# Forgetting attention with a channel mix on one core: a first part of 192 queries, two first chunks of 128 tokens, idle matmuls in vacant banks, one transpose less a head, seven banks at the end

## The chip, the cores and the metric

The kernel runs on one core of one Trainium2 chip. The metric is the device time of one execution in microseconds (us); a kernel's time is the median of several executions. The engines named here are PE (TensorE: matrix products), PEld (its loads of the stationary operand), DVE (VectorE), ACT (ScalarE), POOL (GpSimd) and SP (SyncE, which issues the DMAs).

## What is computed

Causal attention with a forgetting bias for 8 batches, 8 heads, 576 positions and a head size of 64, and then a channel mix over the 512 features of all heads:

```
cum    = cumsum(maximum(s, 0))
scores = where(causal, -1e9, q @ k.T / sqrt(D) + minimum(-(cum_i - cum_j), 0))
attn   = exp(scores - max);  attn = attn / (sum(attn) + 1e-9)
x      = attn @ v                          # as (batch, position, 512)
xk     = mu_k * x + (1 - mu_k) * x_prev    # x_prev: x of the position before
xr     = mu_r * x + (1 - mu_r) * x_prev
k      = maximum(xk @ w_k, 0)              # 512 -> 1024
out    = sigmoid(xr @ w_r) * ((k * k) @ w_v)
```

## The kernel before

**Attention.** The 576 queries of a batch fall into five tiles: tile 0 has 64 queries, tiles 1 to 4 have 128 each, and tile t sees 64, 192, 320, 448 or 576 keys. A *visit* is a pair of heads of one batch with some tiles. Batch 0 is visited in two parts, A (tiles 0, 1, 2: the first 320 queries) for four pairs and then Z (tiles 3, 4) for the four; batches 1 to 7 are visited with all tiles. For each head and tile PE makes the scores in a bank of tag "s" (L667 in plain fp32 in the first four visits; L678 in two passes, with k split into KH and KL, in the rest), DVE adds the bias and reduces (L695, into W), ACT takes the exponent (L713), and POOL normalizes W in place (L726). PE then transposes the normalized weights in pieces of 64 or 128 keys into banks "t" (L772, `turn`), in `block` (a block of 128 keys, all tiles that see them) and `halves` (the 64 keys that tile t alone sees in its own block). ACT and DVE evict them as ph and pl (L799, L803, and L831, L838, L846 for halves). The products with the values (L889 plain for batch 0, L903 split for the others) go to bank "po" and are copied to xT (L924, L931, L935), which is stored to DRAM as x_d.

**Channel mix.** It runs in chunks of CT = 256 tokens, 18 of them. A chunk loads x (L1130), mixes it with the shifted x on ACT and DVE (L977, L986), splits it into xh and xl (L1005, L1009), and makes hidden products with w_k (L1038: four groups of two 128-row blocks of features, 24 matmuls a group), evicted by ACT and DVE as r, a square in place, kh and kl (L1050, L1060, L1065, L1067), then the gate with w_r (L1080, sigmoid L1092) for each 128 tokens, and the output with w_v (L1105, product with the gate L1116, store). `mix(0)` makes xk for the hidden products, `mix(1)` xr for the gate. Each of these products takes a bank of tag "m".

**Banks.** PSUM has eight banks of 512 columns: m 2, t 2, s 2, po 1, and one (xp) for other use.

**Order.** Nothing is emitted as the code above is called. Each call of `pe`, `act`, `dve`, `pool` and `dma` records a task with its engine, a cost, its reads and writes and a due time (class `Plan`). `forward` places the tasks in a list schedule: of the engines' ready tasks the one that starts next and is due first. `backward` makes due times from the schedule, and after some passes the best order is emitted as it is, so each engine's instructions are in a fixed order that the planner chose. Batch 0's early chunks become due as soon as their tokens are there, so the planner fills PE with mix products between the attention's.

**Idle matmuls.** Where the planner sees PE with nothing to do for more than `GAP`, it puts in matmuls that compute nothing (L359: the identity in bf16, 128x192, into columns 320:512 of one "s" bank). They stand until the first split score product (`plan.busy_from`).

Of the kernel before, what the change touches and what calls it, by code (L numbers as in the profile page):

```python
# [14 lines left out]
BF16 = mybir.dt.bfloat16  # L15
# [38 lines left out]
class Plan:  # L54
# [10 lines left out]
    TICK, ENOUGH = 10240 / 3, 3400.0  # L65
    GAP = 170.0

# [53 lines left out]
    def forward(self, due):  # L121
# [11 lines left out]
        engines = {t[0] for t in self.tasks}  # L133
        free = dict.fromkeys(engines, 0.0)
        coming = {e: [] for e in engines}
        ready = {e: [] for e in engines}
# [7 lines left out]
        def clock(s):  # L144
            return 1.0 if ticks.get(int(s // self.TICK) - 1, 0.0) >= self.ENOUGH else 2.0

        def count(s, ns, x):
            while ns > 0.0:
                k = int(s // self.TICK)
                part = min(ns, (k + 1) * self.TICK - s + 1e-3)  # L150
                ticks[k] = ticks.get(k, 0.0) + x * part / ns
                s, x, ns = s + part, x - x * part / ns, ns - part

        while len(order) < n:
            best = None
# [11 lines left out]
            if (  # L167
                waiting
                and f <= s
                and not (ready["PE"] or coming["PE"] and coming["PE"][0][0] < f + self.GAP)  # L170
            ):
                emits.setdefault(len(order), []).append(self.idle)
                ns = 82.0 * clock(f)
                count(f, ns, 192.0)
                free["PE"] = f + ns
                continue
# [108 lines left out]
def forgetting_attention_then_channel_mix(  # L285
# [22 lines left out]
    NF = DF // P  # L308
    CT = 256
    NCHUNK = B * S // CT  # L310
    SCALE = 1.0 / math.sqrt(D)
# [38 lines left out]
    def dma(emit, reads, writes, ns):  # L350
# [5 lines left out]


    idle = bank(1, "s", 2)
    plan.idle = lambda: nc.tensor.matmul(  # L359
        idle.get()[:, 320:512],  # L360
        ident.ap.bitcast(BF16)[:, 0:P],
        ident.ap.bitcast(BF16)[:, 0:192],
        start=True,
# [11 lines left out]

    early = [w[:3] for w in weights]
    for w in weights:
        early.append([])
        for t in range(3):
            c = sum(KN[:t])  # L380
            early[-1].append(fixed(w[NQ - 1].ap[:, c : c + KN[t]]))
        w[NQ - 1].last = early[-1]

    for w in early:
        nc.gpsimd.memset(w[0].ap[64:P], 0.0)

# [157 lines left out]

    ALL, A, Z = tuple(range(NQ)), (0, 1, 2), (3, 4)
    first = []
# [78 lines left out]
    def scores(b, h, tiles, G, KH, KL):  # L625
# [35 lines left out]
        def products(t, m, i, k0, w, W):  # L661
# [14 lines left out]
            for x, K in enumerate((KH, KL) if KL is not None else ()):  # L676
                y = pe(
                    lambda x=x, K=K: nc.tensor.matmul(  # L678
                        ps.get()[:m, :w],
                        G.get()[:, q0 : q0 + m],  # L680
                        K.get()[:, k0 : k0 + w],
                        start=x == 0,
                        stop=x == 1,
                    ),
                    [(G, x) for x in range(2)] + [(K, x) for x in range(2)], [ps], w, m,
                )
                if plan.busy_from is None:
                    plan.busy_from = y

# [33 lines left out]

        def normalize(t, m, n, W):
            pool(
                lambda: nc.gpsimd.tensor_scalar(  # L726
                    out=W.ap[:m, :n],
                    in0=W.ap[:m, :n],
                    scalar1=rinv.get()[:m, t : t + 1],
                    scalar2=1.0,  # L730
                    op0=ALU.mult,
                    op1=ALU.mult,
                ),
                [rinv], [(W, i) for i in range(3)], n, 244,
            )
# [19 lines left out]
        dve(lambda: nc.vector.reciprocal(rs(rinv), rs(rinv)), [], [rinv], 8 * len(tiles))  # L755
        for t in tiles:
            normalize(t, QN[t], KN[t], pt[t])
        return pt

    def weighted(j, pt, V, xT, tiles, plain):  # L760
# [55 lines left out]
        def halves(ps, at, k0, k1):  # L816


            for t in range(k0, k1 + 1):
                turn(ps, at + P * (t - k0), t, t * P, 64)  # L820
            n = 64 * (k1 + 1 - k0)
# [33 lines left out]
        if len(tiles) == NQ:  # L855
            ps = bank(1, "t", 2)
            halves(ps, 0, 1, NQ - 1)
            ps = bank(1, "t", 2)
            block(ps, 0, 0)
            ps = bank(1, "t", 2)  # L860
            halves(ps, 384, 0, 0)
            block(ps, 0, 1)
            ps = bank(1, "t", 2)
            block(ps, 0, 2)
            block(ps, 256, 3)
            rest = ps
        elif tiles[0] == 0:
            ps = bank(1, "t", 2)
            halves(ps, 256, 0, 0)
            block(ps, 0, 0)  # L870
            ps = bank(1, "t", 2)
            halves(ps, 0, 1, 2)
            block(ps, 256, 1)
        else:
            ps = bank(1, "t", 2)
            block(ps, 0, 0, 2)
            ps = bank(1, "t", 2)
            block(ps, 0, 2)
            ps = bank(1, "t", 2)
            halves(ps, 0, 3, 4)  # L880
            block(ps, 256, 3)
        lo, ot = 64 * j, 64 * (1 - j)
# [72 lines left out]

    def channel_mix(ch, start, span):
        t0 = ch * CT
        segs = []
        t = t0
        while t < t0 + CT:  # L960
# [3 lines left out]
            t = e  # L964
        st = {}

        def at(x):
# [29 lines left out]
        def splits(c, xm, hi, lo):  # L997
# [3 lines left out]
            def src():  # L1001
                return xm.get().rearrange("p (c x) -> p c x", c=2)

# [21 lines left out]
        def hidden(fp):  # L1025
# [3 lines left out]
            hi, lo = st[0]  # L1029
            ps = bank(1, "m", 2)  # L1030
            for u in range(2):
                f = 2 * fp + u
                for c in range(NC):
                    for n, (w, x) in enumerate(
                        ((0, hi), (0, lo), (1, hi))
                    ):
                        pe(
                            lambda u=u, f=f, c=c, n=n, w=w, x=x: nc.tensor.matmul(  # L1038
# [6 lines left out]
                            [(weight["k", c, f // 4], w), (x, c)], [ps], CT,  # L1045
                        )

            r = sbuf([P, 2, CT], "r")
            act(
                lambda: nc.scalar.activation(r.get(), ps.get(), AF.Relu, scale=0.5),  # L1050
                [ps], [r], 2 * CT,
            )
            fs = slice(2 * fp, 2 * fp + 2)
            kh, kl = st["kh"], st["kl"]

            def sq():
                return ps.get().rearrange("p (u x) -> p u x", u=2)

            dve(
                lambda: nc.vector.scalar_tensor_tensor(  # L1060
# [12 lines left out]
        def gate(tt):  # L1073
            hi, lo = st[1]
            ts = slice(tt * P, (tt + 1) * P)
            ps = bank(1, "m", 2)
            for c in range(NC):
# [19 lines left out]
        def output(tt):  # L1097
            kh, kl = st["kh"], st["kl"]
            ts = slice(tt * P, (tt + 1) * P)
            ps = bank(1, "m", 2)  # L1100
            for f in range(NF):
# [52 lines left out]

    EARLY = QS[3]
    visits = [(0, hp, x) for x in (A, Z) for hp in range(NP)]
# [80 lines left out]
    for n, (b, hp, tiles) in enumerate(visits):  # L1237
# [19 lines left out]
        while done_chunks < NCHUNK:  # L1257
            end = (done_chunks + 1) * CT - 1
            if end % S >= there[end // S]:
                break  # L1260

            chunk_due = max(chunk_due + CHUNK, due + 2 * step + (MARGIN if end >= S else EARLY_MARGIN))
            channel_mix(done_chunks, chunk_due, CHUNK)
            done_chunks += 1
# [40 lines left out]
```

## Time and profile before

| | us |
|---|---|
| median of 3 runs (lowest, highest) | 902.78 (902.77, 905.7) |
| the profiled execution | 903.98 |
| its span | 902.2 |
| PE busy in the span | 877.5 (97%) |
| ACT busy | 679.4 (75%) |
| DVE busy | 672.1 (74%) |
| POOL busy | 493.5 (55%) |
| hidden products on PE, xh part (L1038) | 233.7 |
| transposes on PE (L772) | 184.1 |
| idle matmuls on PE (L359) | 20.6 |

The profile is of one execution, and the span runs from the first instruction to the last. 1.8 us of the execution lie outside it. An engine's busy time is the union of its instructions' time. Matmuls overlap in PE's pipeline, so a group's mean duration is more than its pace; the pace is read from how far the starts of neighbours stand apart. The chain that ended last is 32% PE, 5% each DVE and ACT; the rest of the span lies before the part that the profile follows back.

### The profile page before, as it was taken

Reading aid. Unit: us, or ns where it says so; the run is one execution under the profiler, and the core shown is the slowest. Engines: PE = TensorE matmul, PEld = TensorE weight load, DVE = VectorE, ACT = ScalarE, POOL = GpSimd, SP = SyncE. Lnnn points to the kernel's source line nnn. Section 1 sums busy time; section 2 is a strip of 40 time slices with the busy share of each in tenths; the row PEclk is TensorE's granted clock in tenths of the full one; section 3 lists DMA queues with packets and bytes.
Section 4 is the critical chain, followed back from the end, with each engine's and each line's share of the span. In section 5 each row is a group of like instructions: output and inputs, shape, how many; then the busy total and the mean of one; then the engine's idle time right before and its main releaser. Section 6 shows DMA issues by size and latency. Waiting matters only on the chain. (4 is left out here: it accounts for less than half of the span.)

```text
span 902.2 us, 18627 instructions
## 1 busy us (share of the span) xinstructions
PE 877.5 (97%) x5664; PEld 760.2 (84%) x5664; DVE 672.1 (74%) x2385; ACT 679.4 (75%) x1810; POOL 493.5 (55%) x856
## 2 busy tenths in 40 slices
PE   8889999999999999999999999999999999998998
PEld 6658778888889898989898989898888888887886
DVE  6887979979877888778878686877777778445431
ACT  4888989989978897789868687877787877335331
POOL 4796998896666576457666466554655551100000
PEclk9999999999999999999999999999999999999999
DMA  7688745563453354234443334342534220101100
GB/s 255 197 254 248 231 136 166 148 174 99 149 154 112 124 144 131 87 97 142 131 130 112 111 109 150 100 127 78 154 81 142 81 85 15 42 31 36 47 24 23
DMA packets 63637, 109.59 MB, mean 121 GB/s; under 512 B 10160, under 2 KB 25008, under 8 KB 63536
## 3 DMA queue, kind: packets, MB, share of 16 engines
q1 hardware_dynamic: 63536, 108.40, 40.0%
q8 instruction: 44, 0.72, 0.3%
q14 instruction: 57, 0.47, 0.2%
HBM read 89.33 MB, written 19.04 MB: 120 GB/s over the span
## 5 line engine op out<-in xcount | busy, mean ns | idle before, releaser
L1038 PE MATMUL m<-xh,w_k 128*128 128x256 f32 x1152 | 233.7, 288 | 2.6 <-DVE kl L1067 2.4
L713 ACT ACTIVATE W<-W,nm 64x64 f32<-64x64 f32 (+4 forms) x320 | 179.7, 562 | 41.8 <-DVE nm L695 35.6
L1105 PE MATMUL m<-w_v,kh 128*128 128x512 f32 x576 | 198.2, 403 | 0.0
L1038 PEld LDWEIGHTS m<-xh,w_k 128*128 128x128 f32 x1152 | 186.7, 190 | 5.4 <-DVE kl L1067 3.1
L772 PE MATMUL t<-ident,W 128*128 128x128 f32 (+1 forms) x960 | 184.1, 276 | 6.4 <-POOL W L726 2.2
L726 POOL TENSOR_SCALAR W<-W,rinv 64x64 f32<-64x64 f32 (+4 forms) x320 | 164.6, 532 | 18.7 <-DVE rinv L755 15.9
L1038 PE MATMUL m<-xl,w_k 128*128 128x256 f32 x576 | 164.9, 286 | 0.1
L772 PEld LDWEIGHTS t<-ident,W 128*128 128x128 f32 (+1 forms) x960 | 112.6, 131 | 35.4 <-DVE pl L803 6.8
L607 POOL TENSOR_TENSOR KL<-raw,KH 128x576 fp32r<-128x576 f32 x64 | 91.7, 1433 | 71.6 <-ACT KH L603 70.2
L1105 PEld LDWEIGHTS m<-w_v,kh 128*128 128x128 f32 x576 | 106.7, 189 | 18.0 <-DVE r L530 0.2
L678 PE MATMUL s<-KH,G 128*64 128x64 f32 (+2 forms) x360 | 113.1, 322 | 4.9 <-DVE nm L695 4.3
L803 DVE TENSOR_TENSOR pl<-t,ph 128x512 fp32r<-128x512 f32 x224 | 106.1, 482 | 15.6 <-ACT ph L799 14.5
L1105 PE MATMUL m<-w_v,kl 128*128 128x512 f32 x288 | 116.8, 406 | 0.0
L695 DVE CUSTOM_DVE_ANT_0 W<-s,cb 128x64 f32<-128x64 f32 (+3 forms) x256 | 94.4, 375 | 28.0 <-PE s L678 19.9
L1038 PEld LDWEIGHTS m<-xl,w_k 128*128 128x128 f32 x576 | 109.4, 190 | 1.3 <-DVE xl L1009 0.3
L986 DVE SCALAR_TENSOR_TENSOR xp<-x,mu,xp 128x256 f32<-128x256 f32 (+3 forms) x192 | 80.6, 420 | 39.0 <-ACT xp L977 36.3
L678 PE MATMUL s<-KL,G 128*64 128x64 f32 (+2 forms) x360 | 108.0, 302 | 0.0
L618 POOL TENSOR_TENSOR G<-raw,G 64x576 fp32r<-64x576 f32 (+1 forms) x64 | 85.8, 1340 | 32.5 <-issue 24.3
L799 ACT CAST ph<-t 128x512 fp32r<-128x512 f32 x224 | 93.3, 422 | 12.6 <-PE t L772 10.9
L1080 PE MATMUL m<-w_r,xh 128*128 128x512 f32 x288 | 102.2, 407 | 0.2
L977 ACT ACTIVATE xp<-x,mu 128x256 f32<-128x256 f32 (+3 forms) x192 | 81.4, 424 | 26.8 <-DVE xl L1009 9.6
L695 DVE CUSTOM_DVE_ANT_0 W<-s,mask,nm 128x128 f32<-128x128 f32 x256 | 86.5, 343 | 5.6 <-PE s L359 1.6
(104 smaller groups left out, 1761.2 us busy)
## 6 DMA issues: line engine op xcount, KB each, us to landing
raw<-in_k SPq DMA_DIRECT2D x128, 144.0 KB, 3.4
cb<-cum_d SPq DMA_DIRECT2D x64, 288.0 KB, 3.7
raw<-in_q SPq DMA_DIRECT2D x112, 144.0 KB, 3.7
out<-g SPq DMA_DIRECT2D x36, 256.0 KB, 2.5
vn<-in_v SPq DMA_DIRECT2D x28, 320.0 KB, 3.8
x_d<-xT SPq DMA_DIRECT2D x28, 288.5 KB, 2.4
x<-x_d SPq DMA_DIRECT2D x12, 514.0 KB, 4.0
w_k<-in_moe_w_k SPq DMA_DIRECT2D x8, 512.0 KB, 6.3
```

The costliest lines, as they stand in the source:

```text
L607: lambda k=k, kh=kh, kl=kl: nc.gpsimd.tensor_tensor(out=kl.get(), in0=k.get(), in1=f32(kh.get()), op=ALU.subtract),
L618: lambda q=q, g=g: nc.gpsimd.tensor_tensor(out=g.get()[64:P], in0=q.get()[64:P], in1=f32(g.get()[64:P]), op=ALU.subtract),
L678: lambda x=x, K=K: nc.tensor.matmul(ps.get()[:m, :w], G.get()[:, q0 : q0 + m], K.get()[:, k0 : k0 + w], start=x == 0, stop=x == 1,),
L695: lambda a=a, e=e, bias=bias, i=i: nc.vector.tensor_tensor_reduce(out=W.ap[:m, a:e], in0=ps.get()[:m, a - k0 : e - k0], in1=bias.get()[:m, ...
L713: lambda: nc.scalar.activation(W.ap[:m, :n], W.ap[:m, :n], AF.Exp, bias=nm.get()[:m, 3 * t + mi : 3 * t + mi + 1], scale=-1.0, accum_out=s ...
L726: lambda: nc.gpsimd.tensor_scalar(out=W.ap[:m, :n], in0=W.ap[:m, :n], scalar1=rinv.get()[:m, t : t + 1], scalar2=1.0, op0=ALU.mult, op1=AL ...
L772: lambda: nc.tensor.transpose(ps.get()[0:m, place : place + P], pt[t].ap[:, k0 : k0 + m], ident.ap),
L799: act(lambda: nc.scalar.copy(strips(ph), src()), [ps], [(ph, k) for k in ks], n * m)
L803: lambda: nc.vector.tensor_tensor(out=strips(pl), in0=src(), in1=f32(strips(ph)), op=ALU.subtract),
L1038: lambda u=u, f=f, c=c, n=n, w=w, x=x: nc.tensor.matmul(ps.get()[:, u * CT : (u + 1) * CT], weight["k", c, f // 4].get()[:, w, f % 4 * P : ...
L1080: lambda c=c, n=n, x=x, w=w: nc.tensor.matmul(ps.get(), x.get()[:, c, ts], weight["r", c, 0].get()[:, w], start=c == 0 and n == 0, stop=c ...
L1105: lambda f=f, n=n, x=x, w=w: nc.tensor.matmul(ps.get(), x.get()[:, f, ts], weight["v", f, 0].get()[:, w], start=f == 0 and n == 0, stop=f ...
```

## The change

1. Part A holds tiles 0 and 1 (192 queries), part Z tiles 2, 3 and 4. `EARLY`, the position to which part A fills x_d, follows.
2. The first chunk of 256 tokens becomes two of 128; 17 of 256 follow. A chunk of 128 has the same number of hidden matmuls, each with half the columns, and one gate and one output product.
3. Idle matmuls have 256 columns and go into any bank of po, s and t that the planner holds to be vacant at that time; the gap that calls for them is 250 ns, and they stand until the first hidden product of the channel mix. In the planner SP is not free before 2000 ns.
4. POOL writes the normalized 64x64 weights of tile 0 into tile 1's weights, in the 64 rows and 64 columns there that are masked for these queries (zero). The transpose of tile 1's half then carries both, so tile 0's half has no transpose of its own, and tile 0 is normalized last. The blocks and halves are spread over the banks "t" in another way.
5. After the last visit the products of the channel mix (hidden, gate, output) take seven banks in turn, m, m, t, t, s, s, po, where they took the two of m. These are the chunks that the last visit completes: the last three.

```diff
-    GAP = 170.0
+    GAP, IDLE = 250.0, ("po", "s", "t")
+
+    FIRST = 2000.0
...
+        free["SP"] = self.FIRST
...
+        banks = [[us[k::len(p)], 0] for p, us in (self.slots[x] for x in self.IDLE) for k in range(len(p))]
+
+        def vacant(f):
+            for x in banks:
+                us = x[0]
+                while x[1] < len(us) and all(done[i] and done[i] + 400.0 <= f for i in us[x[1]].tasks):
+                    x[1] += 1
+                if x[1] == len(us) or not any(done[i] for i in us[x[1]].tasks):
+                    return us[0]
+            return None
...
                 and not (ready["PE"] or coming["PE"] and coming["PE"][0][0] < f + self.GAP)
+                and (x := vacant(f))
             ):
-                emits.setdefault(len(order), []).append(self.idle)
-                ns = 82.0 * clock(f)
-                count(f, ns, 192.0)
+                emits.setdefault(len(order), []).append(lambda x=x: self.idle(x))
+                ns = 108.0 * clock(f)
+                count(f, ns, 256.0)
...
-    CT = 256
-    NCHUNK = B * S // CT
+    CHUNKS = [P, P] + [2 * P] * (B * S // (2 * P) - 1)
+    NCHUNK = len(CHUNKS)
...
-    idle = bank(1, "s", 2)
-    plan.idle = lambda: nc.tensor.matmul(
-        idle.get()[:, 320:512],
+    plan.idle = lambda x: nc.tensor.matmul(
+        x.get()[:, 0:256],
         ident.ap.bitcast(BF16)[:, 0:P],
-        ident.ap.bitcast(BF16)[:, 0:192],
+        ident.ap.bitcast(BF16),
...
-    ALL, A, Z = tuple(range(NQ)), (0, 1, 2), (3, 4)
+    ALL, A, Z = tuple(range(NQ)), (0, 1), (2, 3, 4)
...
         def normalize(t, m, n, W):
+            to, c = (pt[1], P) if t == 0 else (W, 0)
             pool(
                 lambda: nc.gpsimd.tensor_scalar(
-                    out=W.ap[:m, :n],
+                    out=to.ap[:m, c : c + n],
                     in0=W.ap[:m, :n],
...
-                [rinv], [(W, i) for i in range(3)], n, 244,
+                [rinv] + [(W, i) for i in range(3)], [(to, i) for i in range(3)], n, 244,
...
-        for t in tiles:
+        for t in sorted(tiles, key=lambda t: (t == 0, t)):
             normalize(t, QN[t], KN[t], pt[t])
...
         def halves(ps, at, k0, k1):
-            for t in range(k0, k1 + 1):
-                turn(ps, at + P * (t - k0), t, t * P, 64)
+            if k0:
+                for t in range(k0, k1 + 1):
+                    turn(ps, at + P * (t - k0), t, t * P, 64)
+                if k0 == 1:
+                    halves(ps, at, 0, 0)
...
+    LATE = [("m", 2), ("m", 2), ("t", 2), ("t", 2), ("s", 2), ("s", 2), ("po", 1)]
+    late = [0]
...
+        def product():
+            if not after:
+                return bank(1, "m", 2)
+            late[0] += 1
+            return bank(1, *LATE[late[0] % len(LATE)])
...
-            ps = bank(1, "m", 2)
+            ps = product()
...
+                        if plan.busy_from is None:
+                            plan.busy_from = i
...
-    EARLY = QS[3]
+    EARLY = QS[2]
...
-            channel_mix(done_chunks, chunk_due, CHUNK)
+            channel_mix(done_chunks, chunk_due, CHUNK, n == len(visits) - 1)
```

In the rows of order below, an entry is the line, the operation, the tile written and the tiles read; a digit behind a tile's name is the buffer (s0, s1), and the last number is only a running one.

The first place is on PE around the first hidden product of the channel mix. In the kernel before it follows part Z's scores and transposes of tiles 3 and 4:

```order
L772 MATMUL t1_339<-ident_66,W3_0_74 128x128
L772 MATMUL t1_339<-ident_66,W4_0_75 128x128
L678 MATMUL s0_99<-KH2_597,G2_591 128x288
L678 MATMUL s1_179<-KL1_670,G2_591 128x448
L678 MATMUL s0_99<-KL1_670,G2_591 128x288
L772 MATMUL t0_333<-ident_66,W3_0_74 64x128
L772 MATMUL t0_333<-ident_66,W4_0_75 64x128
L1038 MATMUL m0_199<-xh00_958,w_k_0_00_269 128x256
```

In the changed kernel the same place on PE reads:

```order
L375 LDWEIGHTS ident_66
L375 MATMUL po0_95<-ident_66 128x256
L691 MATMUL s0_210<-KH1_537,G1_440 128x320
L691 MATMUL s0_210<-KL0_562,G1_440 128x320
L786 MATMUL t1_356<-ident_66,W4_1_80 128x128
L786 MATMUL t0_320<-ident_66,W4_1_80 128x128
L1065 MATMUL m0_185<-xh00_895,w_k_0_00_245 128x128
L1065 MATMUL m0_185<-xl00_905,w_k_0_00_245 128x128
```

An idle matmul now stands shortly ahead of it, in bank po; the hidden product has 128 columns where it had 256; and part Z's scores of tile 2, split in two passes (L691 with 320 columns), stand beside it. Ahead of the first hidden product there are 24 plain score products, 74 transposes, 34 plain value products, 28 split score products and 168 idle matmuls in the order of before, and 16, 34, 16, 26 and 257 in that of the change.

The second place is on PE in part A. Before, all idle matmuls go to s0, which real scores use too (here W of tiles 2 and 0 of the second head):

```order
L359 LDWEIGHTS ident_66
L359 MATMUL s0_99<-ident_66 128x192
L667 MATMUL s1_179<-KH0_139,G0_132 128x320
L359 LDWEIGHTS ident_66
L359 MATMUL s0_99<-ident_66 128x192
...
L667 MATMUL s0_99<-KH0_139,G0_132 64x64
```

In the change, on PE in part A:

```order
L375 MATMUL t0_320<-ident_66 128x256
L786 MATMUL t1_356<-ident_66,W1_1_77 64x128
L680 MATMUL s0_210<-KH2_261,G2_249 64x64
L375 LDWEIGHTS ident_66
L375 MATMUL t0_320<-ident_66 128x256
L375 LDWEIGHTS ident_66
L375 MATMUL po0_95<-ident_66 128x256
```

The idle matmuls change between t0 and po, as these come free in the plan.

The third place is on ACT in the first of the last three chunks (r and kh are the evictions of hidden products; xp and xh belong to the second mixing, for the gate). Before:

```order
L1050 ACTIVATE r0_1067<-m0_199 128x512
L1005 CAST xh10_1058<-xp0_307 128x512
L1065 CAST kh0_1093<-m0_199 128x512
L1050 ACTIVATE r0_1067<-m1_289 128x512
L1065 CAST kh0_1093<-m1_289 128x512
L977 ACTIVATE xp0_307<-x0_890,mu_86 128x256 x2
```

In the changed kernel, on ACT in the same chunk:

```order
L1085 ACTIVATE r0_1017<-m0_185 128x512
L1094 CAST kh0_1031<-m0_185 128x512
L1085 ACTIVATE r0_1017<-t0_320 128x512
L1094 CAST kh0_1031<-t0_320 128x512
L1085 ACTIVATE r0_1017<-t1_356 128x512
L1094 CAST kh0_1031<-t1_356 128x512
L1085 ACTIVATE r0_1017<-s0_210 128x512
L1032 CAST xh00_895<-xp0_296 128x512
L1094 CAST kh0_1031<-s0_210 128x512
```

The four hidden products of the chunk stand in four banks, and the two chunks behind it go on through s1, po, m and t. The second mixing's last cast stands ahead of the first eviction in the change, and inside it before.

More of the change, by code (lines that the diff above doesn't have):

```diff
@@ L374, in forgetting_attention_then_channel_mix @@
     ]
-    early = [w[:3] for w in weights]
+    early = [w[:2] for w in weights]
     for w in weights:
         early.append([])
-        for t in range(3):
+        for t in range(2):
             c = sum(KN[:t])
@@ L382, in forgetting_attention_then_channel_mix @@
         w[NQ - 1].last = early[-1]
-    for w in early:
-        nc.gpsimd.memset(w[0].ap[64:P], 0.0)
     STEP = S - P
@@ L676, in products @@
             for x, K in enumerate((KH, KL) if KL is not None else ()):
-                y = pe(
+                pe(
                     lambda x=x, K=K: nc.tensor.matmul(
@@ L686, in products @@
                 )
-                if plan.busy_from is None:
-                    plan.busy_from = y
             for a, e in ((k0, min(k0 + w, QS[t])), (max(k0, QS[t]), k0 + w)):
@@ L860, in weighted @@
             ps = bank(1, "t", 2)
-            halves(ps, 384, 0, 0)
             block(ps, 0, 1)
@@ L868, in weighted @@
             ps = bank(1, "t", 2)
-            halves(ps, 256, 0, 0)
+            block(ps, 0, 0)
+            halves(ps, 128, 1, 1)
+        else:
+            ps = bank(1, "t", 2)
             block(ps, 0, 0)
             ps = bank(1, "t", 2)
[L872 to L876, printed above, removed]
+            block(ps, 0, 1)
             ps = bank(1, "t", 2)
@@ L879, in weighted @@
             ps = bank(1, "t", 2)
-            halves(ps, 0, 3, 4)
-            block(ps, 256, 3)
+            halves(ps, 0, 2, 4)
+            block(ps, 384, 3)
         lo, ot = 64 * j, 64 * (1 - j)
@@ L954, in forgetting_attention_then_channel_mix, with channel_mix @@
     x_d = [fixed(dram.tile([P, NP, S + 1], F32, name=f"x_d{b}")) for b in range(B)]
-    def channel_mix(ch, start, span):
-        t0 = ch * CT
+    LATE = [("m", 2), ("m", 2), ("t", 2), ("t", 2), ("s", 2), ("s", 2), ("po", 1)]
+    late = [0]
+    def channel_mix(ch, start, span, after):
+        CT = CHUNKS[ch]
+        t0 = sum(CHUNKS[:ch])
         segs = []
@@ L1001, in src @@
             def src():
-                return xm.get().rearrange("p (c x) -> p c x", c=2)
+                return xm.get()[:, 0 : 2 * CT].rearrange("p (c x) -> p c x", c=2)
             act(
@@ L1036, in hidden @@
                     ):
-                        pe(
+                        i = pe(
                             lambda u=u, f=f, c=c, n=n, w=w, x=x: nc.tensor.matmul(
@@ L1046, in hidden @@
                         )
+                        if plan.busy_from is None:
+                            plan.busy_from = i
             r = sbuf([P, 2, CT], "r")
[L1049 to L1052, printed above, removed]
             fs = slice(2 * fp, 2 * fp + 2)
@@ L1056, in sq @@
             def sq():
-                return ps.get().rearrange("p (u x) -> p u x", u=2)
+                return ps.get()[:, 0 : 2 * CT].rearrange("p (u x) -> p u x", u=2)
+            act(
+                lambda: nc.scalar.activation(r.get(), sq(), AF.Relu, scale=0.5),
+                [ps], [r], 2 * CT,
+            )
             dve(
@@ L1075, in gate @@
             ts = slice(tt * P, (tt + 1) * P)
-            ps = bank(1, "m", 2)
+            ps = product()
             for c in range(NC):
@@ L1099, in output @@
             ts = slice(tt * P, (tt + 1) * P)
-            ps = bank(1, "m", 2)
+            ps = product()
             for f in range(NF):
@@ L1257, in forgetting_attention_then_channel_mix @@
         while done_chunks < NCHUNK:
-            end = (done_chunks + 1) * CT - 1
+            end = sum(CHUNKS[: done_chunks + 1]) - 1
             if end % S >= there[end // S]:
```

## The prediction

> **What bounds the kernel now.** I read the busy share by stretch first, because one average would mix the start, the long middle and the end. Columns: stretch and its length, busy time (and instructions) of PE, its weight loads, DVE, ACT and POOL, the granted TensorE clock, the DMA share, GB/s.
>
> ```profile
> 0.00:10.00 10.00, 8.03 (x68) 7.24 (x69) 4.79 (x8) 2.66 (x3) 4.17 (x28) 1.00 0.71 247
> 10.00:20.00 10.00, 8.73 (x72) 6.21 (x69) 6.94 (x31) 5.92 (x18) 3.72 (x11) 1.00 0.83 261
> 20.00:30.00 10.00, 9.20 (x53) 5.82 (x54) 8.51 (x36) 8.88 (x31) 7.42 (x18) 1.00 0.75 211
> 30.00:40.00 10.00, 8.48 (x52) 5.66 (x52) 7.49 (x29) 6.74 (x24) 8.27 (x19) 1.00 0.66 205
> 40.00:50.00 10.00, 9.40 (x62) 7.01 (x61) 9.53 (x37) 9.55 (x33) 8.39 (x17) 1.00 0.65 219
> 50.00:60.00 10.00, 7.84 (x41) 5.10 (x40) 8.92 (x26) 9.34 (x26) 9.04 (x15) 1.00 0.86 264
> 60.00:70.00 10.00, 8.72 (x39) 6.23 (x39) 7.13 (x27) 7.46 (x19) 9.52 (x13) 0.83 0.72 216
> 300.00:400.00 100.00, 99.64 (x663) 87.85 (x662) 79.78 (x299) 81.84 (x226) 62.54 (x102) 1.00 0.43 125
> 800.00:820.00 20.00, 17.60 (x103) 15.82 (x102) 10.85 (x23) 9.79 (x22) 0.00 (x0) 0.94 0.16 54
> 820.00:840.00 20.00, 20.00 (x102) 16.98 (x102) 9.96 (x17) 9.06 (x18) 0.00 (x0) 0.97 0.13 41
> ```
>
> The middle is PE's: 99.64 us busy in 100, with the other four at 63 to 88. So the time is PE's work plus the PE time lost at the two ends, and an edit pays if it takes PE work away or gives PE work earlier. In the first 70 us PE looks busy too, but much of that is the idle matmuls (L359), which compute nothing.
>
> ```profile
> L359 PE MATMUL s<-ident 128*128 128x192 bf16 x168 | 20.6, 262 | 5.5 <-DVE nm L695 3.9 <-POOL ident masks.py:199 1.6
> DVE W L695 <- PE s L359: 6.1, 11, 0.9
> PE s L359 <- DVE nm L695: 3.9, 9, 0.7
> ...
> 8.99 3.13 PE L359 MATMUL s<-ident 128*128 128x192 bf16 x36 [0.32 <-DVE nm L695]
> 30.37 1.06 PE L667 MATMUL s<-KH,G 64*128 64x320 f32 x4
> 72.77 1.03 PE L889 MATMUL po<-ph,V 128*128 128x256 f32 x4
> 89.08 0.60 PE L772 MATMUL t<-ident,W 128*128 128x128 f32 x4
> 71.11 0.48 PE L1038 MATMUL m<-xh,w_k 128*128 128x256 f32 x2
> ```
>
> The last row is the first product of the channel mix, at 71.11 us. Useful PE work ahead of it, counted in program order and priced by these rows: 24 plain score products of 4608 columns at 1.06/640 = 1.66 ns each (the row holds two products of 320 columns, two records to a product), 7.6 us; 74 transposes 0.108 apart ((0.60 - 0.277)/3), 8.0; 34 plain value products of 6656 columns at about the same 1.66 (two products of 256 in 1.03 us with the last drain), 11.0; 28 split products of 9664 columns at 0.48 (from the gate row below, 5.88/(24x512)), 4.6. That is 31.3, so **39.8 us of PE are lost before the mix begins**. The end is in the chain of waits and its list of releasers:
>
> ```profile
> 815.96 0.69 DVE xl L1009
> 816.65 0.61 DVE kl L1067
> ...
> 817.31 7.45 PE m L1038 x48
> 824.75 5.88 PE m L1080 x24
> 841.55 11.63 PE m L1038 x96
> 853.18 5.87 PE m L1080 x24
> ...
> PE m L1038 <- DVE kl L1067: 2.4, 1, 2.4
> PEld m L1080 <- DVE kl L1067: 1.0, 4, 0.3
> ```
>
> PE waits 2.4 us for kl, which frees one of the two m banks but stands on DVE behind the mixing rows of the second half. Then 48 hidden matmuls take 7.45 us, where half of the next chunk's 96 take 5.82: 1.63 more, and the clock column has 0.94 and 0.97 there.
>
> **The change part by part.**
>
> PE work. The 64 transposes of tile 0's half (one a head) go: 64 x 0.108 = -6.9. Plain score products fall from 4608 to 2048 columns, because part Z's scores are split products: 2560 x 1.66 = -4.2, against 2 x 2560 columns at 0.48, +2.4. Two chunks of 128 tokens need 192 hidden matmuls where one of 256 needs 96:
>
> ```profile
> 872.78 0.30 PEld L1038 LDWEIGHTS m<-xh,w_k 128*128 128x128 f32 x2
> ```
>
> Two loads of 0.19 end after 0.30, so they start 0.11 apart, and nowhere in the trace do such loads come closer. At 256 columns a matmul takes 11.63/96 = 0.121. I take 0.108 at 128 columns: 192 x 0.108 - 11.63 = +9.1. The other bound is half of 0.121, 11.6 us for all 192, +0.0. The loads decide, since every hidden matmul has its own. Gate and output keep their 128-token weights: 0. **PE work: -6.9 - 4.2 + 2.4 + 9.1 = +0.4.** The Trainium skill ("TensorE: Matmul & The Clock Gate", LDWEIGHTS (loading the stationary operand)) prices a load by its columns over 1.2, an estimate of 107 ns here, with which the trace agrees; but its section Back-to-back issue gap gives some 81 ns a pair at 128 columns, by which the sum would be 5.2 us lower (192 x 0.027).
>
> The start. Ahead of the first mix product stand, in the changed order, 16 plain score products (2048 columns, 3.4 us), 34 transposes (3.7), 16 value products (2048 columns, 3.4) and 26 split ones (8704, 4.1): 14.6 us in place of 31.3. What moved is done behind it, where PE is the bound, so the start pays only if the first product comes earlier than 71.1 - (31.3 - 14.6) = 54.4. When does it come?
>
> ```profile
> 55.56 0.42 ACT L924 COPY xT<-po 64x320 f32<-64x320 f32 x1
> 61.12 0.59 SPq L1130 DMA_DIRECT2D x<-x_d  x1
> 68.07 0.97 ACT L977 ACTIVATE xp<-x,mu 128x256 f32<-128x256 f32 x2
> 70.74 0.69 DVE L1009 TENSOR_TENSOR xl<-xp,xh 128x512 fp32r<-128x512 f32 x1 [0.39 <-ACT xh L1005]
> ```
>
> The chain is: last output of part A, store, load of x, mixing on ACT and DVE, split, product. DVE is busy 53.3 of the first 70 us.
>
> ```profile
> L695 DVE CUSTOM_DVE_ANT_0 W<-s,mask,nm 128x128 f32<-128x128 f32 x256 | 86.5, 343 | 5.6 <-PE s L359 1.6 <-DVE pl L838 0.3 <-PE t L772 0.3
> L695 DVE CUSTOM_DVE_ANT_0 W<-s,cb 128x192 f32<-128x192 f32 x64 | 22.4, 350 | 5.4 <-PE s L678 3.5 <-PE s L359 0.9 <-PE t L772 0.5
> ```
>
> Ahead of the first xl it has 186 rows before and 149 now, by their groups' means 51.1 and 43.0 us, so -8.1: these two reductions of the third tile for 8 heads are 5.5 of it, the rest is prefix sums, weights and half-width mixing. ACT and POOL lose more. If DVE's idle time stays, xl comes at 70.7 - 8.1 = 62.6; at the same busy share at 59.5. The 6.1 us that reductions wait behind idle matmuls of their own bank should go, since an idle matmul now needs a vacant bank: 56.5 and 54.4 (6.1 at DVE's share of 0.84 is 5.1). Nothing excludes less: PE in order could reach the mix at 45.6 (14.6 of work, 257 idle matmuls of 107 ns, 3.5 us of first waits). **I take 55.0**, near the lower of the two since ACT and POOL are relieved too. Lost: 55.0 - 14.6 = 40.4, **+0.6**; bounds -8.8 (45.6) and +8.2 (62.6).
>
> Behind the first mix product I leave the loss as it is:
>
> ```profile
> 139.38 0.28 PE L1038 MATMUL m<-xh,w_k 128*128 128x256 f32 x1
> ```
>
> The second chunk begins there, 68.3 us later with 60.3 of work, 8.0 lost. The changed order has 59.4 there. DVE's work is equal (51), ACT's 4 larger, POOL's 4 larger; at the same share the second chunk begins at 122.3. What it costs if its tokens, which need part Z, come 3 us later: +3.
>
> The transposes that go also release ACT and DVE behind them. By the prices above PE loses some 17 us between 170 and 740, mostly around banks t; in proportion to 64 of 960 transposes that is **-1.0** (bounds -2.2 and 0).
>
> ```profile
> L772 PEld LDWEIGHTS t<-ident,W 128*128 128x128 f32 x640 | 79.3, 140 | 28.9 <-DVE pl L803 6.8 <-POOL W L726 3.8 <-DVE pl L838 3.0
> L726 POOL TENSOR_SCALAR W<-W,rinv 64x64 f32<-64x64 f32 x64 | 20.0, 312 | 6.5 <-DVE rinv L755 6.3 <-DMA cb<-cum_d 0.2
> ```
>
> Tile 1's half transpose now waits for the 64x64 normalization, 0.31 later on POOL. I cost it at nothing, because POOL runs ahead (62.54 of 100); without that cover PE's wait for W of 3.8 might double, +3.8.
>
> The end. With seven banks for the last three chunks the hidden products need no bank from kl. What is late next is the gate's xh and xl: xl is done at 816.65, and the four hidden products, unbroken, end at 814.8 + 5.8 = 820.6. So the 2.4 goes, the 1.63 of half clock with it, and of the 1.0 of small waits I take 0.6: **-4.6** (bounds 0 and -5.0). The half clock came after a wait of 2.4 us. The Trainium skill (same page, What's actually happening) has the clock halved after an idle window of about 3.4 us; by that rule alone the 2.4 us would not have cost clock, and the term would be -3.0. The row (0.94) decides.
>
> Sum: +0.4 + 0.6 - 1.0 - 4.6 = **-4.6**. The profiled execution took 903.98 with a span of 902.2; it would take 899.4. Against the median shown, 902.78, that is **898.2**.
>
> **The rivals.** A measurement of this kernel tells about 0.5% from no change, 898.3 to 907.3; my sum stands on the lower line.
>
> - **The extra banks only move the end's wait.** The chain of ACT and DVE rows in order is the same, and the second half's mixing stands in it. For: DVE is the releaser. Against: xl is ready 4 us before the gate could want it. Then the end gives 0 to -1: 902.
>
> - **The mix starts late (slower than before).** If DVE keeps its idle time (62.6, behind transfers at 0.65 to 0.86 of the DMA engines, or because ACT's chain from the output to the mixing, 55.56 to 68.07, doesn't shrink), the half-width chunk's 9.1 us are not paid back: 898.2 + 7.6 = 905.8. From a first product at 59.6 the whole is slower than before; at 65 it is 908.
>
> - **Reductions were the brake.** With their waits gone the mix starts at 50: 893.2. For: the 6.1 and 3.9 above. Against: POOL is at 9.04 and 9.52 of 10 just there.
>
> - **Short matmuls are not bound by loads**: half the price, 898.2 - 9.1 = 889.1. The Trainium skill's isolated gap (Back-to-back issue gap) would say about this, an estimate of 56 ns. Against: the 0.11 spacing of loads.
>
> - **The idle matmuls get in the way.** There are 257 in place of 168, and longer. If a score product behind one comes 0.1 us later some 30 times on the path: 901. It is also how the part on vacant banks might not do what it says, as the planner's vacancy need not be the chip's.
>
> **How the numbers follow.** Forecast 0.45 (895 to 901, so 0.27 of it beyond the line), banks 0.15, late mix 0.14 (0.10 of it beyond 907.3), early mix 0.12, short matmuls 0.06, idle matmuls 0.08. Faster by over 0.5%: 0.27 + 0.12 + 0.06 = 0.45. Within: 0.18 + 0.15 + 0.08 + 0.04 = 0.45. Slower: 0.10. The range 890.0 to 905.8 leaves out the short matmuls and the worse part of the late mix.
>
> **What would show it.** First mix product at 54 to 56.5 and none of the reductions waiting for an idle matmul; hidden matmuls of 128 columns 0.108 apart; 896 transposes; the second chunk near 122; at the third chunk from the end no wait for kl and a clock of 1.00 from there on. A first product beyond 60, or a gate waiting for xl, makes it wrong.

## The result, and the profile after

| | us |
|---|---|
| before, median of 4 runs (lowest, highest) | 903.06 (902.77, 905.7) |
| changed, median of 4 runs (lowest, highest) | 916.44 (912.95, 924.84) |
| ratio, 95% interval | 1.0144 (1.0111 to 1.0177) |
| the profiled execution of the change, its span | 924.84, 923.1 |

The change is slower by 13.4 us where I forecast 4.6 less. The profiled execution is the longest of its four: its granted clock is 0.986, that of the others 0.996 to 0.999, so it holds something that the others have little of. The ratios here and below leave out four slow runs: 2158.9 and 1405.3 of the kernel before, 1430.1 of `gaps_before` and 931.2 of `split_only`.

First PE alone in five stretches, before and then changed. The columns are the stretch and its length, PE's busy time and instructions, the granted clock, the DMA share and GB/s.

```profile
0.00:120.00 120.00, 109.14 (x676) 0.99 0.74 227
120.00:160.00 40.00, 39.22 (x267) 1.00 0.54 162
160.00:260.00 100.00, 97.30 (x633) 1.00 0.51 144
260.00:800.00 540.00, 535.88 (x3550) 1.00 0.36 108
800.00:880.00 80.00, 77.60 (x461) 0.98 0.10 34
```

```profile
0.00:120.00 120.00, 114.77 (x752) 1.00 0.78 221
120.00:160.00 40.00, 38.47 (x212) 0.70 0.49 135
160.00:260.00 100.00, 99.13 (x675) 1.00 0.44 131
260.00:800.00 540.00, 525.89 (x3432) 1.00 0.38 110
800.00:880.00 80.00, 79.35 (x489) 1.00 0.12 40
```

Three rows differ most. From 120 to 160 the clock is 0.70, which is 12 us of PE, and PE idles 0.8 more. From 260 to 800 PE is idle for 540 - 525.89 = 14.1 us where it was idle for 4.1. From 800 on it gains 1.75 of idle time and the 0.02 of clock, 1.6. From 160 to 260 it idles 1.8 less. So 12 + 0.8 + 10 - 3.4 - 1.8 = 17.6 of the profiled execution's 20.9. The first row cannot be compared in this way, because the idle matmuls count as busy in it; the rest lies there. A run with the clock up lacks the 12.

Next the stretch of low clock, in windows of 3.41 us of the changed kernel, and PE's timeline inside it.

```profile
120.48:123.89 3.41, 3.17 (x21) 1.00 0.89 198
123.89:127.31 3.42, 2.13 (x15) 0.84 0.77 200
127.31:130.72 3.41, 3.41 (x18) 0.50 0.50 150
...
144.37:147.79 3.42, 3.42 (x17) 0.50 0.00 0
147.79:151.20 3.41, 3.41 (x23) 0.66 0.63 169
151.20:154.61 3.41, 3.41 (x25) 1.00 0.57 182
```

```profile
125.18 0.66 PE L786 MATMUL t<-ident,W 128*128 128x128 f32 x4 [1.53 <-DVE xT L950]
...
130.34 0.63 PE L1065 MATMUL m<-xh,w_k 128*128 128x128 f32 x2
130.77 0.41 PE L1065 MATMUL m<-xl,w_k 128*128 128x128 f32 x1
130.98 0.63 PE L1065 MATMUL m<-xh,w_k 128*128 128x128 f32 x2
...
150.53 0.28 PE L1065 MATMUL m<-xl,w_k 128*128 128x128 f32 x1
150.65 0.39 PE L1065 MATMUL m<-xh,w_k 128*128 128x128 f32 x2
150.87 0.27 PE L1065 MATMUL m<-xl,w_k 128*128 128x128 f32 x1
```

PE waits 1.5 us for a "t" bank, the clock halves, and then it stays at 0.50 for 24 us although PE is never idle (3.41 of 3.41). What runs there are mostly the half chunk's products of 128 columns: three in 0.64 (130.34 to 130.98), 0.213 each, and 0.113 each after 150.5.

Last what PE's weight loads wait for from 260 to 800 us (engine, tile and line, releaser, total us, times, longest), before and then changed.

```profile
PEld s L678 <- DVE nm L695: 7.8, 20, 0.9
PEld t L772 <- DVE pl L803: 4.2, 12, 0.8
PEld t L772 <- DVE pl L838: 2.8, 6, 1.0
PEld po L903 <- ACT ph L799: 1.1, 2, 0.5
...
PEld po L903 <- DVE pl L803: 0.3, 2, 0.2
```

```profile
PEld s L691 <- DVE nm L706: 11.2, 21, 1.5
PEld po L918 <- ACT ph L813: 6.4, 12, 1.2
PEld t L786 <- DVE pl L817: 4.1, 11, 0.6
PEld po L918 <- DVE pl L817: 3.4, 11, 0.6
```

The idle time has no new engine behind it. Scores wait for a bank that DVE has not reduced, about as often as before but longer (11.2 us in place of 7.8). Value products wait for weights that ACT and DVE have not evicted, now 23 times where it was 4. Transposes wait less for pl (4.1 in place of 7.0).

### The profile page after: what moved, and what is told of

Its sections match the earlier page's. It is cut to its first block, busy times and chain, and to the rows that moved or that the text cites. A ratio compares the mean times of both kernels' runs of the same rounds, so it can differ in the third digit from the quotient of the medians.

```text
span 923.1 us, 18866 instructions
## 1 busy us (share of the span) xinstructions
PE 896.7 (97%) x5769; PEld 780.1 (85%) x5769; DVE 678.3 (73%) x2405; ACT 687.5 (74%) x1830; POOL 495.6 (54%) x852
## 4 chain that ended last, share of the span: by engine, by line
PE 34%; ACT 7%; DVE 6%; issue 2%; DMA 1%; POOL 0%; SPq 0%; ACTq 0%; POOLq 0%; DVEq 0%
PE m L1065 9%; PE m L1134 8%; PE t L786 3%; PE s L691 3%; PE po L918 3%; PE m L1109 3%; PE t L1134 2%; DVE W L706 2%; ACT xp L1004 2%; DVE xp L1013 2%; PE s L1065 2%; PE t L1065 1%; ACT W L724 1%; DMA x<-x_d 1%; ACT xh L1032 1%
## 5 line engine op out<-in xcount | busy, mean ns | idle before, releaser
L1065 PE MATMUL m<-xh,w_k 128*128 128x256 f32 (+1 forms) x1040 | 218.1, 292 | 0.0
L724 ACT ACTIVATE W<-W,nm 128x576 f32<-128x576 f32 (+4 forms) x320 | 179.9, 563 | 45.8 <-DVE nm L706 35.0
L1134 PE MATMUL m<-w_v,kh 128*128 128x512 f32 x528 | 185.4, 405 | 0.0
L786 PE MATMUL t<-ident,W 128*128 128x128 f32 (+1 forms) x896 | 170.7, 277 | 6.0 <-DVE xT L950 3.9
L740 POOL TENSOR_SCALAR W<-W,rinv 128x576 f32<-128x576 f32 (+4 forms) x320 | 165.2, 535 | 14.6 <-DVE rinv L769 10.8
L1065 PE MATMUL m<-xl,w_k 128*128 128x256 f32 (+1 forms) x520 | 150.8, 290 | 0.0
L691 PE MATMUL s<-KH,G 128*128 128x288 f32 (+1 forms) x368 | 117.6, 325 | 7.7 <-DVE nm L706 7.4
L706 DVE CUSTOM_DVE_ANT_0 W<-s,cb 128x288 f32<-128x288 f32 (+3 forms) x256 | 95.3, 375 | 22.7 <-PE s L691 15.3
L691 PE MATMUL s<-KL,G 128*128 128x288 f32 (+1 forms) x368 | 111.6, 306 | 0.0
L918 PE MATMUL po<-ph,V 128*128 128x448 f32 x280 | 90.0, 323 | 2.2 <-ACT ph L813 2.1
```

The lines of the kernel that those rows point to most:

```text
L691: lambda x=x, K=K: nc.tensor.matmul(ps.get()[:m, :w], G.get()[:, q0 : q0 + m], K.get()[:, k0 : k0 + w], start=x == 0, stop=x == 1,),
L706: lambda a=a, e=e, bias=bias, i=i: nc.vector.tensor_tensor_reduce(out=W.ap[:m, a:e], in0=ps.get()[:m, a - k0 : e - k0], in1=bias.get()[:m, ...
L724: lambda: nc.scalar.activation(W.ap[:m, :n], W.ap[:m, :n], AF.Exp, bias=nm.get()[:m, 3 * t + mi : 3 * t + mi + 1], scale=-1.0, accum_out=s ...
L740: lambda: nc.gpsimd.tensor_scalar(out=to.ap[:m, c : c + n], in0=W.ap[:m, :n], scalar1=rinv.get()[:m, t : t + 1], scalar2=1.0, op0=ALU.mult ...
L786: lambda: nc.tensor.transpose(ps.get()[0:m, place : place + P], pt[t].ap[:, k0 : k0 + m], ident.ap),
L918: lambda: nc.tensor.matmul(po.get()[: P if both else 64, at + q0 - base : at + q0 - base + m], V.get()[:, kb, 2 * j : 2 * j + (2 if both e ...
```

## The experiments

Each theory has a letter in what was expected: S, the split of parts 1 and 2 is the cause; M, the merged transposes of part 4; P, any new order of the planner; C and W, two views of the clock; T, an order that asks for evictions too soon. S2 and M2 are their second forms.

Each kernel was timed beside runs of the kernel before on the same chip; the ratio is to those. "Idle" is PE's idle time between 260 and 800 us in the profile, read as above.

| kernel | median us | ratio (95%) | idle, us |
|---|---|---|---|
| before | 903.1 to 906.2 by set of runs | 1 | 4.1 |
| changed | 916.4 | 1.0144 (1.0111 to 1.0177) | 14.1 |
| no_turn: all but part 4 | 914.2 | 1.0102 (1.0069 to 1.0135) | 8.4 |
| no_split: all but parts 1, 2 | 905.8 | 0.9997 (0.9974 to 1.0020) | 13.2 |
| turn_only: part 4 | 901.4 | 0.9960 (0.9941 to 0.9980) | 7.6 |
| late_only: part 5 | 902.2 | 0.9975 (0.9957 to 0.9994) | 4.4 |
| idle_late: parts 3, 5 | 897.7 | 0.9925 (0.9897 to 0.9952) | 6.3 |
| turn_late: parts 4, 5 | 898.2 | 0.9937 (0.9917 to 0.9956) | 8.4 |
| split_only: parts 1, 2 | 917.3 | 1.0158 (1.0125 to 1.0192) | |
| chunks_only: part 2 | 917.2 | 1.0147 (1.0118 to 1.0177) | 6.1 |
| A_only: changed, chunks of 256 | 918.6 | 1.0136 (1.0109 to 1.0163) | 10.9 |
| pad: changed, 256 columns streamed | 915.6 | 1.0124 (1.0102 to 1.0146) | 13.8 |
| replan: before, another order | 909.7 | 1.0052 (1.0030 to 1.0075) | 7.8 |
| gaps_before: before, longer gaps planned | 902.7 | 0.9966 (0.9947 to 0.9985) | 6.2 |
| gaps_turn: no_split, longer gaps | **888.8** | 0.9828 (0.9798 to 0.9859) | 4.1 |
| gaps_after: changed, longer gaps | 897.4 | 0.9905 (0.9872 to 0.9937) | 5.0 |

### Which part: four kernels

`no_turn` is the change with tile 0's own transpose and `normalize` as before; `no_split` has

```diff
-    CHUNKS = [P, P] + [2 * P] * (B * S // (2 * P) - 1)
+    CHUNKS = [2 * P] * (B * S // (2 * P))
-    ALL, A, Z = tuple(range(NQ)), (0, 1), (2, 3, 4)
+    ALL, A, Z = tuple(range(NQ)), (0, 1, 2), (3, 4)
-    EARLY = QS[2]
+    EARLY = QS[3]
```

with the blocks of A and Z spread for those tiles; `turn_only` is before with part 4; `replan` is before with one number of the planner altered:

```diff
-    MARGIN = 25000.0
+    MARGIN = 26000.0
```

> The changed kernel with part 4 taken back (tile 0's half is transposed by itself, 960 transposes, tile 0 normalized first). In the profile of the change PE loses some 14 us more than before between 300 and 800 us, with new waits for xT (L950), ph and nm. Theory M (the merged transposes make that middle): it goes, 916.4 - 14 + 7 for the transposes = 907 to 910, and PE's waits for nm, xT and ph between 260 and 750 fall from about 11 to under 4. Theory S (the split into 192 queries and half chunks shifts the chunks and makes it): 916 to 923, the waits stay. Theory P (any new order of the planner draws the middle anew): anything from 903 to 920, waits not tied to this part.

> The changed kernel with parts 1 and 2 taken back (part A of 320 queries, 18 chunks of 256). The half clock from 124 to 150 us stood over the 128-column hidden products of the second chunk; the start lost 5 us more. Theory S: all of it goes, 897 to 901, clock 0.99 or more. Theory M: the start and the half clock go but the middle stays: 908 to 911. Theory P: the half clock goes for certain (clock 0.996 or more, runs within 1 us of each other), the rest anything from 897 to 912.

> The kernel before with part 4 alone. Theory M: 903 - 7 + 14 = 908 to 911, with new waits for xT and nm in the middle. Theory S: the 64 transposes less are a plain gain, 896 to 899. Theory P: 896 to 910, by the draw.

> The kernel before with one due-time constant of the planner altered (MARGIN 25000 to 26000): the same work, another order. Theories M and S: 902 to 904, since no work differs. Theory P: it moves by over 3 us, up or down, and the loss of PE between 260 and 750 us (11 before) changes by as much.

Measured: 914.2, 905.8, 901.4 and 909.7. Theory S falls as put, since without the split the middle still idles 13.2 us; the split costs 1.5% by other means (1.0144 against 0.9997, some 13 us). Theory M falls as put: part 4 alone is a gain of 0.4%, not a loss. But it is not free of idle time: 64 transposes less, 6.9 us by their pace, bring 0.2 to 0.6%, and PE idles 3.5 more. The time of `no_turn` is no clean price of part 4: its granted clock is 0.989 to 0.992 in all four runs, some 7 to 10 us, in stretches of half clock that its profile has between 33 and 64 us. Theory P holds in `replan`: with no work changed, another order costs 0.5% (0.3 to 0.75) and 3.7 us more idle. One altered order shows that orders differ, not how widely.

### The clock: a program by itself, and a padded kernel

`probe` computes nothing of the reference: it runs streams of products with a pause of 15 us before each. `pad` has the order of the change, instruction for instruction; only the half chunks' hidden products stream their columns twice:

```diff
-                                ps.get()[:, u * CT : (u + 1) * CT],
+                                ps.get()[:, 256 * u : 256 * u + 256],
...
-                                x.get()[:, c, :],
+                                x.get()[:, c, :] if CT == 256 else x.get()[:, c : c + 1, :].broadcast_to([P, 2, CT]),
```

> A program by itself that computes none of the reference's output: streams of products on PE, each after about 10 us in which PE is idle: 120 of 256 columns, 200 of 128, 60 of 256, 200 transposes of 128x128, 160 of 192, 60 of 512, every one with its own load of 128 columns. Theory C (the clock comes back only where columns stream most of the time, and loads don't count): the 256 and 512 streams run at half clock for at most two windows of 3.4 us and then at 1.00; the 128 stream stays at 0.50 for its whole length (about 200 x 0.21 = 43 us), the transposes too. Rival W (any busy PE brings it back, the 24 us in the change had another cause): all streams reach 1.00 after 3.4 to 7 us, the 128 stream then at 0.108 each.

> The changed kernel in the very same order, but the hidden products of the two 128-token chunks stream each column twice (256 columns into the bank, the second 128 read by nobody). Cost at full clock: 192 x (0.121 - 0.108) = +2.5 us. Theory C: no stretch of half clock longer than 7 us in any chunk, the clock of all runs 0.995 or more, so 912 to 917 and a smaller spread than the 12 us between the change's runs. Rival W: runs with a clock under 0.99 remain, median 917 to 921.

PE's timeline of `probe` shows the streams (start, length, shape, count); windows of 4 us give the clock (fourth number).

```profile
49.70 42.93 PE L314 MATMUL ps<-w 128*128 128x128 f32 x200 [15.38 <-DVE w L306]
108.01 9.14 PE L314 MATMUL ps<-w 128*128 128x256 f32 x60 [15.38 <-DVE w L306]
132.15 23.78 PE L312 MATMUL ps<-ident,b 128*128 128x128 f32 x200 [15.01 <-DVE b L305]
171.31 20.68 PE L314 MATMUL ps<-w 128*128 128x192 f32 x160 [15.38 <-DVE w L306]
```

```profile
52.00:56.00 4.00, 4.00 (x21) 0.50 0.00 0
...
88.00:92.00 4.00, 4.00 (x20) 0.50 0.00 0
...
108.00:112.00 4.00, 3.99 (x19) 0.52 0.01 4
112.00:116.00 4.00, 4.00 (x36) 1.00 0.00 0
...
132.00:136.00 4.00, 3.85 (x19) 0.53 0.00 0
136.00:140.00 4.00, 4.00 (x39) 1.00 0.00 0
...
172.00:176.00 4.00, 4.00 (x21) 0.50 0.02 4
176.00:180.00 4.00, 4.00 (x35) 0.91 0.00 0
```

The stream of 128 columns never gets the clock back: 42.93/200 = 0.215 each to its end, with PE busy throughout. Products of 256 columns stand as far apart at half clock (19 in 4 us) and have it back after about 4 us, those of 192 after 5 to 6 (the row at 176 us has 0.91). So a busy PE alone does not bring the clock back, and rival W falls. Theory C, that it counts how much of the time columns stream, fits the three widths: at half clock a product of 128 columns takes as long as one of 256. It does not fit the transposes, which I had put with the 128-column products: they too stand 0.20 apart at first (19 in 3.85 us), and they have the clock back within 4 us. They also differ in type, fp32 where the products are fp32r. What exactly the clock counts stays open. The Trainium skill ("TensorE: Matmul & The Clock Gate", Part 4: PE-mode transpose) says that full rate does not engage for transposes; for these, fp32 and 128x128, the row at 136 us has 1.00.

`pad` came to 915.6 in runs from 914.4 to 916.7 at clocks from 0.998 to 1.00, with no window of half clock in its profile. By my estimate it streams 2.5 us more, and still it lies 0.8 below the change's median, and the long tail (924.84) is gone. Four runs a side cannot price the tail, and in the profile of `pad` the wait ahead of the half chunk (1.07 us where the change has 1.53) did not lower the clock, so it shows no recovery either. That a half chunk can hold the clock down for most of its length is shown by the probe and the change's own trace together. The profile of `split_only`, its 931.2 run, has such a stretch too: 0.50 from 133 to 160 us, over the second half chunk.

### The split, part by part

`split_only` and `late_only` are before with those parts alone, `chunks_only` has `CHUNKS` of the change and part A as before, `A_only` is the change with the chunks of before.

> The kernel before with parts 1 and 2 alone (192 queries, two chunks of 128). PE work +7.3 (hidden +9.1, plain scores -4.2, split +2.4). Theory S2 (the split costs its PE work and pays back nothing because the mix starts only 10 us earlier with 17 us less done ahead of it): 905 + 7 + 3 = 913 to 918. If the early start paid for the loads: 902 to 906.

> The kernel before with part 5 alone (seven banks for the last three chunks). My sum's term: the wait for kl and the half clock near 815 go, -4.6: 899 to 902. Rival (the draw of the planner decides as much as the part): the loss between 780 and 900 us falls from 6.5 to 2 as the term says, but the whole is anything from 897 to 908.

> The kernel before with the first chunk split in two of 128 tokens, part A still 320 queries. PE work +9.1, and a half-width mixing lets the first hidden product start at 64 to 68 in place of 71: lost time ahead of it 3 to 6 less. Theory S2: 903 + 9 - 4 = 907 to 910. If the short products find the clock low: runs with clocks under 0.99 and a spread of over 5 us, 910 to 918.

> The changed kernel with 18 chunks of 256 tokens, so part A holds 192 queries but the first chunk needs part Z. PE work 9.1 less than the change. If the half chunks are the whole price of the split (chunks_only +12.5, split_only +12 to 14): 902 to 907, beside 905.8 without the split. If the early mix was worth something: the first hidden product comes at 75 or later and the time is 908 to 914.

By the ratios each half of the split alone is as dear as both: +1.5% the chunks, +1.4% part A (against `no_split`, 918.6 to 905.8). `chunks_only` came out 7 us above what I expected: the first hidden product comes at 69.6 in place of 71.1, too little to pay for the work of +9.1, and its order is worse too (PE busy for 105.8 of the first 120 us in place of 109.1, idle 6.1 in place of 4.1). `A_only` lies above both of my ranges. It has its first hidden product at 113.5 us, since a chunk of 256 tokens must wait for part Z when part A has 192. But of its 13 us over `no_split`, 9.4 are one wait, at its first output product:

```profile
149.25 0.79 PE L1134 MATMUL m<-w_v,kh 128*128 128x512 f32 x1 [9.41 <-DVE r L543]
```

PE stands still until DVE is done with the bank m, in which it is still making w_v; the clock is at half behind it. `no_split` waits 0.3 us at that line. So `A_only` prices its own order more than part A. What stays is that an early mix needs part 2 with part 1, and that part 2 costs 9 us of PE.

`late_only` is without kl's wait at 815, and from 800 to 880 PE is busy for 79.35 us in place of 77.60. The whole gains 0.25% (0.06 to 0.43), 2.3 us, which is half of the term's 4.6.

### The order: parts 3 to 5, and longer gaps

`idle_late` has parts 3 and 5, `turn_late` parts 4 and 5. The `gaps_` kernels change one line of the planner, the time that it puts between the end of an instruction and the start of one on another engine that needs it:

```diff
-    AFTER = {"PE": 235.0, "ACT": 150.0, "DVE": 160.0, "POOL": 60.0, "SP": 1000.0}
+    AFTER = {"PE": 235.0, "ACT": 250.0, "DVE": 260.0, "POOL": 60.0, "SP": 1000.0}
```

> The kernel before with parts 3 and 5 alone (idle matmuls in vacant banks, seven banks at the end). PE loses from 260 to 800 us: 12.5 before, 14.2 with part 5 alone, 18.8 with part 4 alone, 27.3 with 3, 4 and 5. Theory M2 (the transposes taken away come back as waits, since value products and transposes follow too soon on their evictions): 13 to 17 here, time 900 to 903. Theory P (any new order draws the middle anew): 12 to 27, no relation to part 4; above 20 speaks for P.

> Parts 4 and 5 alone, without the split and with the idle matmuls of before. If the parts add: before - 4.0 (part 4) - 2.0 (part 5) = 898 to 900, faster than both kernels. If part 5's and part 3's new order lost the 4.5 us between turn_only (901.4) and no_split (905.8) for part 5's sake: 903 to 906.

> Parts 3, 4 and 5 (the kernel of no_split, 905.8), with the planner told that what follows ACT and DVE on another engine starts 100 ns later than it assumed. The work is the same. Theory T (the middle is lost because the order asks for evictions sooner than the chip has them): PE's loss from 260 to 800 falls from 27 to 10 to 16, the waits of po for ph (7.3) and s for nm (14) at least halve, time 893 to 900. Rival (the extra waits are a matter of throughput of ACT and DVE, not of order): loss 24 to 30, time 904 to 908.

> The changed kernel with the planner told of 100 ns more behind ACT and DVE. Theory T: the loss from 260 to 800 falls from 27 to 10 to 14, time 916 - 15 = 898 to 903; it stays 9 to 14 above gaps_turn (888.8), which is the split's own price. Rival: the early mix fills the middle in another way and the loss stays over 20: 910 to 917.

> The kernel before with the planner told the same. Its middle loses 12.5, of which waits for nm and pl are 16 on the load side. Theory T with the order as one cause for all kernels: the loss falls to 8 to 11, time 898 to 902, so parts 3 to 5 still give gaps_turn 9 to 13. Rival (most of gaps_turn's gain over the kernel before is the order's): 890 to 895.

PE's load side waits as follows from 260 to 800 us, with PE's row for the stretch, first in `no_split` and then in `gaps_turn`.

```profile
PEld s L691 <- DVE nm L706: 9.7, 20, 1.2
PEld po L918 <- ACT ph L813: 5.7, 11, 1.2
```

```profile
260.00:800.00 540.00, 526.84 (x3452) 1.00 0.36 106
```

```profile
PEld s L691 <- DVE nm L706: 3.0, 8, 0.9
PEld po L918 <- DVE pl L817: 1.7, 4, 0.5
PEld po L918 <- ACT ph L813: 0.9, 3, 0.5
```

```profile
260.00:800.00 540.00, 535.94 (x3526) 1.00 0.36 107
```

Theory T holds: with the same work as `no_split` and only another order, the waits for nm fall from 9.7 to 3.0 and those of po for ph from 5.7 to 0.9, the idle time from 13.2 to 4.1, and the time by 1.7% (0.9828 against 0.9997), some 15 us. That is more than the 9.1 of idle time. PE counts as busy while a matmul's modelled end runs out, so idle time shows a part of the loss only: in these 540 us PE has 3526 matmuls on record in place of 3452, and 3525 weight loads in place of 3452. 888.8 is below both kernels. In the change itself the same line takes the idle time from 14.1 to 5.0 and the time from 916.4 to 897.4. The rival, a lack of throughput in ACT or DVE, falls: both have the same work. Both kernels with much idle time gained in the waits that T names; that longer gaps mend any order is not shown by that. In the kernel before, the line gains 0.3% (0.15 to 0.5) and no idle time: its order stood well already, so parts 3, 4 and 5 are worth 1.4% (0.9828 against 0.9966) once the order lets them. `turn_late` added up as forecast. `idle_late`, 897.7, was 2 below what I expected, and its first hidden product comes at 66.3 where it came at 71.1.

The two `gaps_` kernels with and without the split stand 897.4 to 888.8, in separate sets of runs; by their ratios the split costs 0.8%, some 7 us (3 to 11 by the two intervals). I had expected 9 to 14 there; it is the work that my sum has for it: 9.1 - 4.2 + 2.4 = 7.3.

## Why the prediction was wrong

**PE work, +0.4: right.** There are 896 transposes and 192 products of 128 columns, at 0.113 each where I took 0.108, so 1 us more. The rival of short matmuls at half the price is out.

**The start, +0.6: off by 3.** In the changed trace

```profile
58.02 0.31 PE L1065 MATMUL m<-xh,w_k 128*128 128x128 f32 x1
```

the first hidden product comes at 58.0, not 55.0; by my own break-even of 54.4 a loss of 3.6. Reductions no longer wait for idle matmuls (0.3 us are left of 6.1), but they wait for other things in their place:

```profile
DVE W L706 <- PE s L680: 2.6, 3, 2.0
DVE W L706 <- POOL mask L662: 1.5, 3, 0.7
DVE W L706 <- DMA cb<-cum_d: 1.3, 2, 0.7
...
DVE W L706 <- PE po L375: 0.3, 1, 0.3
```

That is 5.7 us, where before they waited 6.1 for idle matmuls and 0.9 for scores. So most of the saving that I counted in full was not there. The stretch behind it went as put: the second chunk began 67.6 us later (125.59; I had 67.3). The early mix pays back nothing that `gaps_after` against `gaps_turn` can show: there the split costs 7 us (3 to 11), and its work is 7.3.

**The later slack, -1.0: the step that failed.** I took a loss in proportion to the transposes and gave it bounds of -2.2 and 0. It came out as +10.0 (idle 4.1 to 14.1). The sum treated the order as given and priced only the work in it, but every part of the change makes the planner draw a new order for all 900 us, and the trace of before could not show how well a new one would fit. `replan` shows that an order may cost 0.5% by itself, `gaps_turn` and `gaps_after` that some 9 us of this idle time belong to the order and not to the parts. Where the kernels have the longer gaps, the other terms come out: the change stands 0.6% (0.2 to 1.0) below the kernel before (0.9905 against 0.9966), some 5.5 us where I forecast 4.6. The split costs 7 and parts 3 to 5 give 12 to 13 (the 1.4%); my terms for them add up to +7.9 (with the start's 0.6) and -12.5. Why parts 3, 4 and 5 together drew an order with more idle time than parts 4 and 5 (13.2 against 8.4) is not settled, nor which of the planner's times is too short on the chip.

**The end, -4.6: right in kind, 3.4 in size.** The wait for kl at the third chunk from the end and the half clock behind it are gone. In their place stand, from 780 us on,

```profile
PE m L1109 <- DVE kl L1096: 0.7, 1, 0.7
PE t L1065 <- ACT xh L1032: 0.7, 1, 0.7
```

one wait for kl in the chunk before the rotation begins, and one for the mixing. The rival in which the banks only move the wait is out.

**The half clock: not among the terms.** I saw it twice in the trace of before, each time for one window, and counted it as something that a stall costs and that then ends. There products of 256 columns followed. With a half chunk behind the stall it lasted 24 us, 12 us of time in the profiled execution. By the clocks of the others (0.996 to 0.999) it is 1 to 4 us, no more than in the kernel before (0.996), so it makes the tail and not the median. Without it the measured terms add up to 1.4 + 3.6 + 10.0 - 3.4 = 11.6, against the 13.4 of the medians.

The rival of a late mix had the right sign by another road, and its price was of work that the early start does not pay back, which is what remains (7 us) when the order is mended.

## What to carry to other kernels

Where a scheduler writes the order, an edit's price has two parts, its work and the new order; time the old kernel under one altered constant first, to know how much an order is worth, and try the change with the scheduler's latencies lengthened before judging it (here 916.4 became 897.4, and without the split 888.8). Cutting a chunk in half bought next to nothing on PE here, since each product loads its own weights: 0.113 us a product of 128 columns, 0.121 of 256. And if the clock has dropped, such short products can hold it down for as long as they run (43 us in the probe).

## What was not expected of the hardware

Busy is not enough for the clock: PE at 4.00 us in 4 stayed at 0.50 for 43 us with products of 128 columns, and came back within about 4 us with 256, 5 to 6 with 192, and 4 with fp32 transposes of 128. A wait of 1.5 us, in a stretch in which PE was busy for 2.13 of 3.42, was enough to lose it in one execution; a wait of 1.07 us in `pad` was not.
